# Moving exponentials, transposes and a split of maxima in the first batch of an mLSTM and Fourier-mixing kernel

## The chip, the cores and the metric

The kernel runs on one core of a Trainium2 chip. The metric is device microseconds of one execution. Single executions of this kernel on one core have no neighbour to be compared with, so all runs quoted are those that the measurement calls fast (none was called slow); the granted clock of TensorE is quoted beside a time where it matters. It is the mean over the span, 1.0 being full speed.

## The reference

The kernel computes two blocks in a row: an mLSTM cell over 768 tokens, and a Fourier mixing block with a two-layer MLP.

```python
B, H, S, D = 4, 8, 768, 40                       # d_model = H * D = 320
for t in range(S):                               # mLSTM cell
    m_new  = np.maximum(f_gate[:, :, t] + m, i_gate[:, :, t])
    f_stab = np.exp(f_gate[:, :, t] + m - m_new)
    i_stab = np.exp(i_gate[:, :, t] - m_new)
    C = f_stab * C + i_stab * outer(v_t, k_t)
    n = f_stab * n + i_stab * k_t
    y[:, :, t] = sigmoid(o_gate_t) * (C @ q_t) / np.maximum(np.abs(n @ q_t), 1.0)
# ... heads are joined: x is (4, 768, 320)
mixed = np.real(np.fft.fft(np.fft.fft(x, axis=1), axis=2))
u  = x + mixed
un = (u - mean(u)) / np.sqrt(var(u) + 1e-06)
out = u + np.maximum(un @ w_ch1, 0.0) @ w_ch2
```

## The kernel before

The mLSTM is computed in chunks of 128 tokens, six for each of the four batches. Within a chunk the recurrence becomes products: a chunk's output is (queries times the state C of the chunks before) plus (a 128x128 matrix of weighted scores times the values), and the state C is then carried on. The order in which each engine's instructions are issued is a hand-made plan: `at(slot, phase, function, ...)` puts a function at a slot, and within a slot smaller phases come first (`FILL` is 1, `FILL_PE` is 3). In the first batch (b = 0) chunk c begins at slot 3c.

```python
def spread_max(b, c, h0):            # TensorE: maxima and mask of four heads into PSUM, pM
    ...
def mlstm_exp(b, c, h0):             # ScalarE: four exponentials, W <- pM
    for h in range(h0, h0 + NP):
        nc.scalar.activation(out=k.W[:, h, :], in_=M, func=AF.Exp, scale=-1.0, bias=...)
def mlstm_scores(b, c): ...          # TensorE: ps
def mlstm_weigh(b, c): ...           # VectorE: W <- ps * W
def mlstm_from_state(b, c): ...      # TensorE: ph <- qg, C   ("state products")
def mlstm_from_chunk(b, c): ...      # TensorE: ph <- W, values
def mlstm_to_state(b, c): ...        # TensorE: pc, what the chunk adds to C
def mlstm_gather(b, c):              # ScalarE: the copies
    for hip in range(2):
        nc.scalar.copy(out=Cv, in_=k.pc[r])          # C of the next chunk, b == 0
    nc.scalar.copy(out=k.hT[r], in_=k.ph[r])         # h (cut: reversed and shifted forms)
    nc.scalar.activation(out=k.so, in_=k.so, func=AF.Tanh, scale=0.5)
def mlstm_turn(b, c, early): ...     # TensorE: transposes of h, px
def mlstm_finish(b, c): ...          # VectorE: x of the chunk, from px
# ...
def parts(s):                        # the split of the maxima into three bf16 parts, M3
    m, rest_ = M[0:BH, s], shift[:, s]
    nc.scalar.copy(out=M3[0:BH, s], in_=m)
    nc.vector.tensor_tensor(out=rest_, in0=m, in1=M3[0:BH, s], op=OP.subtract)
    nc.scalar.copy(out=below[:, s], in_=rest_)
    nc.scalar.copy(out=M3[BH:2 * BH, s], in_=rest_)
    nc.vector.tensor_tensor(out=M3[2 * BH:, s], in0=rest_, in1=below[:, s], op=OP.subtract)
# ...
def idle_products(n, ps=ps_s, tag="ps"):   # scratch products that only keep TensorE busy
    pw = ps.tile([L, 2 * L], FP, name="pi", tag=tag)
    for i in range(n):
        nc.tensor.matmul(pw, rest[:, 0:L], rest, start=True, stop=True, skip_group_check=True)
# ... the plan of a batch (cut)
at(s, FILL, mlstm_exp, b, c, 0)
at(s + 1, FILL - 0.5, mlstm_exp, b, c, NP)
at(s, FILL_PE + 2, mlstm_scores, b, c)
at(s + 2, FILL, mlstm_weigh, b, c)
at(s + 3, FILL_PE, mlstm_from_state, b, c)
at(s + 3, FILL_PE + 3, mlstm_from_chunk, b, c)
at(s + 3, FILL_PE + 3, mlstm_to_state, b, c)
at(s + 4, FILL, mlstm_gather, b, c)
```

After the chunks, `mix_fold` (VectorE, tile fe) and `mix_seq` (TensorE, tile pz) begin the Fourier transform. Pieces of the MLP's weights are converted along the way (`take`, `convert`, `join`, of which `convert` is ScalarE's, tiles e and m).

## Time and profile before

| | before |
|---|---|
| time, median of 4 runs | 463.84 us (463.58 to 464.18) |
| profiled run, another execution | 465.65 us, span 463.9 us, mean granted clock 0.985 |
| end of the first batch's mLSTM: last pz of part 0, profiled run | 60.23 us |
| mean granted clock of runs near 463.8 us (13 of 25 in the later calls) | 0.991 to 0.993 |
| half clock before 70 us, profiled run | 10.24 us, from 18.51 |

In the views PE is TensorE, PEld its weight loads, ACT ScalarE, DVE VectorE and POOL GpSimd; L470 is line 470 of the kernel. The page of the kernel before has these two rows: TensorE's busy tenths and the tenths of full clock granted, in 40 slices of 11.6 us.

```profile
PE   8688679999899999999999899999999999999997
PEclk9779999999999999999999989999999999999999
```

But for two eights and the last slice, all of TensorE's row that is not 9 lies in the first six slices, and slices two and three have a lowered clock.

The timeline of TensorE (columns: start us, busy us, engine, line, operation, tiles, form, count) gives the rhythm of the state products: 21.16, then 30.93, 37.49 and 44.04.

```profile
21.16 2.02 PE L470 MATMUL ph<-qg,C 128*128 128x128 f32 x8
30.93 1.11 PE L470 MATMUL ph<-qg,C 128*128 128x128 f32 x8
37.49 1.11 PE L470 MATMUL ph<-qg,C 128*128 128x128 f32 x8
44.04 1.11 PE L470 MATMUL ph<-qg,C 128*128 128x128 f32 x8
60.23 1.56 PE L631 MATMUL pz<-ds_sb,fe 128*128 128x385 f32 x4 [0.93 <-DVE fe L596]
```

The first group takes 2.02 us and the others 1.11 us for the same eight products: that is the half clock of chunk 1. What ScalarE does at a turn-around shows in its own timeline. The eight exponentials of chunk 2 are done long before the copies, so the copies of C start the moment pc is there (the bracket is ScalarE's own idle time, which costs nothing here):

```profile
22.03 2.18 ACT L412 ACTIVATE W<-pM,colT 128x128 f32<-128x128 f32 x8
28.20 0.62 ACT L502 COPY C<-pc 40x164 f32<-40x164 f32 x2 [4.00 <-PE pc L492]
28.84 0.59 ACT L515 COPY h<-ph 128x512 f32<-128x512 f32 x1
```

### The profile page before, as it was taken

What the parts mean: (1) busy time and instruction counts of PE and PEld (TensorE: products, weight loads), DVE (VectorE), ACT (ScalarE), POOL (GpSimd) and SP (SyncE); (2) the same over time, 40 slices, a digit from 0 to 9 for tenths busy, and PEclk for the clock granted to TensorE, in tenths of its full rate; (3) what the DMA queues carried; (4) which work ended last, traced back from release to release, by engine and by line L of the source; (5) the groups of instructions that cost most, each with busy time, mean ns of one, the idle gap of its engine ahead of it and who ended that gap; (6) DMA issues with size and microseconds to landing.
All of it is one profiled execution on the core that took longest, in us unless ns stands there. A gap on an engine that the chain in (4) does not pass through costs nothing.

```text
span 463.9 us, 7230 instructions
## 1 busy us (share of the span) xinstructions
PE 440.3 (95%) x2710; PEld 291.1 (63%) x2710; DVE 226.4 (49%) x582; ACT 154.7 (33%) x415; POOL 87.9 (19%) x129
## 2 busy tenths in 40 slices
PE   8688679999899999999999899999999999999997
PEld 6576435576567777766665467775664566466464
DVE  8568776859994336576301753346501640130110
ACT  7857247665442232352003442234001210200100
POOL 4344101434531431022001044302000000000000
PEclk9779999999999999999999989999999999999999
DMA  7488926259455244000067134300000000000000
GB/s 241 139 267 284 288 82 198 70 191 297 125 155 167 60 145 144 29 1 2 14 200 229 66 87 144 107 12 1 14 30 1 0 15 30 0 14 30 0 14 28
DMA packets 19566, 45.49 MB, mean 98 GB/s; under 512 B 2588, under 2 KB 9116, under 8 KB 19404
## 3 DMA queue, kind: packets, MB, share of 16 engines
q1 hardware_dynamic: 19532, 45.04, 31.2%
q8 instruction: 21, 0.34, 0.3%
q14 instruction: 13, 0.11, 0.1%
HBM read 40.92 MB, written 4.11 MB: 97 GB/s over the span
## 4 chain that ended last, share of the span: by engine, by line
PE 84%; DVE 8%; ACT 3%; issue 3%; POOL 1%; DMA 1%; POOLq 0%; ACTq 0%; DVEq 0%
PE po L783 28%; PE pm L761 21%; PE pm L765 6%; PE ps L456 4%; PE ph L477 4%; PE pu L662 4%; PE ph L470 4%; PE pz L631 3%; PE px L526 2%; PE put L702 2%; PE pzt L631 1%; PE pc L487 1%; PE pM L210 1%; DVE W L462 1%; ACT W L412 1%
## 5 line engine op out<-in xcount | busy, mean ns | idle before, releaser
L783 PE MATMUL po<-w_sb,hT 128*128 128x320 f32 x480 | 133.5, 435 | 0.0
L761 PE MATMUL pm<-uT,w_sb 128*128 128x384 f32 x320 | 119.1, 503 | 1.2 <-ACT uT L707 0.6
L783 PEld LDWEIGHTS po<-w_sb,hT 128*128 128x128 f32 x480 | 89.9, 190 | 39.4 <-issue 3.5
L761 PEld LDWEIGHTS pm<-uT,w_sb 128*128 128x128 f32 x320 | 56.9, 192 | 40.6 <-issue 10.1
L789 DVE SCALAR_TENSOR_TENSOR ot<-po,rstd,u 128x320 f32<-128x320 f32 x24 | 13.2, 551 | 84.0 <-PE po L783 84.0
L773 DVE TENSOR_SCALAR hT<-pm 128x384 f32<-128x384 f32 x35 | 19.4, 555 | 60.4 <-PE pm L765 60.1
L775 ACT ACTIVATE hT<-pm 128x384 f32<-128x384 f32 x45 | 21.5, 491 | 77.7 <-PE pm L765 77.7
L412 ACT ACTIVATE W<-W,colT 128x128 f32<-128x128 f32 x144 | 44.9, 395 | 0.0
L434 POOL TENSOR_SCALAR_AFFINE_SELECT W<-W 128x1024 f32<-128x1024 f32 x18 | 20.5, 1138 | 98.1 <-ACT W L412 68.0
L765 PE MATMUL pm<-uT,w1t_sb 64*128 64x384 f32 x160 | 36.6, 535 | 0.0
L707 ACT COPY uT<-put 128x384 f32<-128x384 f32 x24 | 11.5, 479 | 67.2 <-PE put L702 67.1
L462 DVE TENSOR_TENSOR W<-ps,W 128x512 f32<-128x512 f32 x48 | 30.7, 680 | 5.8 <-POOL W L434 5.7
L456 PE MATMUL ps<-qk 40*128 40x128 f32 x384 | 29.1, 290 | 0.4 <-DVE W L462 0.3
L456 PEld LDWEIGHTS ps<-qk 40*128 40x128 f32 x384 | 24.6, 193 | 5.0 <-issue 1.2
L422 POOL TENSOR_TENSOR qg<-qk,Gb 128x512 f32<-128x512 f32 x19 | 26.2, 1380 | 3.6 <-DMA Gb<-G_d 3.5
L477 PE MATMUL ph<-W,kvt 128*41 128x128 f32 x384 | 26.7, 283 | 0.0
L765 PEld LDWEIGHTS pm<-uT,w1t_sb 64*128 64x128 f32 x160 | 12.0, 184 | 21.8 <-issue 21.8
L470 PEld LDWEIGHTS ph<-qg,C 128*128 128x128 f32 x160 | 20.9, 198 | 5.8 <-issue 2.6
L428 POOL TENSOR_TENSOR vw<-kvt,colT 128x328 f32<-128x328 f32 x20 | 16.8, 840 | 36.2 <-DMA kvt<-in_kv 29.4
L470 PE MATMUL ph<-qg,C 128*128 128x128 f32 x160 | 22.9, 288 | 0.3 <-DVE x L541 0.3
L477 PEld LDWEIGHTS ph<-W,kvt 128*41 128x41 f32 x384 | 20.1, 120 | 3.1 <-issue 0.2
L526 PE MATMUL px<-ident,h 128*128 128x128 f32 x96 | 15.0, 279 | 4.8 <-ACT h L519 2.8
(140 smaller groups left out, 467.7 us busy)
## 6 DMA issues: line engine op xcount, KB each, us to landing
W<-M_d SPq DMA_DIRECT2D x18, 512.0 KB
kvt<-in_kv SPq DMA_DIRECT2D x24, 324.0 KB
qk<-in_qkT SPq DMA_DIRECT2D x48, 160.0 KB
raw<-in_w SPq DMA_DIRECT2D x10, 640.0 KB
so<-in_o SPq DMA_DIRECT2D x24, 160.0 KB
out<-ot SPq DMA_DIRECT2D x24, 160.0 KB
Gb<-G_d SPq DMA_DIRECT2D x38, 80.0 KB
ds_sb<-in_dft_s SPq DMA_DIRECT2D x1, 1155.0 KB
```

What stands on the lines that cost most here:

```text
L412: nc.scalar.activation(out=k.W[:, h, :], in_=M, func=AF.Exp, scale=-1.0, bias=colT[:, c, 0, b * H + h:b * H + h + 1])
L422: nc.gpsimd.tensor_tensor(out=k.qg, in0=k.qk[:, 0], in1=k.Gb, op=OP.mult)
L434: nc.gpsimd.affine_select(out=W, in_=W, compare_op=OP.is_ge, fill=0.0, base=0, pattern=[[0, H], [1, L]], channel_multiplier=-1)
L456: nc.tensor.matmul(k.ps[hip][:, p, :], k.qk[r, 1, p, :], k.qk[r, 0, p, :], start=True, stop=True)
L462: nc.vector.tensor_tensor(out=Wv, in0=k.ps[hip], in1=Wv, op=OP.mult)
L470: nc.tensor.matmul(k.ph[:, p, :], k.C[:, p, :], k.qg[:, p, :], start=(p == 0), stop=False, skip_group_check=True)
L477: nc.tensor.matmul(k.ph[hip * 64:hip * 64 + D1, p, :], k.v1[:, 2 * p + hip, :], k.W[:, 2 * p + hip, :], start=(c == 0 and p == 0), stop=Tr ...
L526: nc.tensor.transpose(k.px[:, p, :], k.hT[:, p, :], ident)
L761: nc.tensor.matmul(k.pm[i], w1_sb[:, ch, f0:f0 + L], u[2 * ch], start=(ch == 0), stop=False)
L765: nc.tensor.matmul(k.pm[i], w1t_sb[r, f // 2 * L:(f // 2 + 1) * L], u[1][r], start=False, stop=True)
L775: nc.scalar.activation(out=ht, in_=k.pm[f % 2], func=AF.Relu, scale=-1.0)
L783: nc.tensor.matmul(k.po, k.h[gr][f][:, i * L:(i + 1) * L], w2_sb[:, f, :], start=(f == 0), stop=(f == NFF - 1))
```

## The change

The intent is to use ScalarE's idle time under a chunk's products: the exponentials of a later chunk are put ahead of the copies, with two weight conversions; the transposes px go behind the next chunk's products and x behind the weighing, so that neither stands in front of work that the next products need; and the split of the maxima goes behind the exponentials of chunk 1, so that TensorE gets its first decays (pd) sooner. The arithmetic is the same, only order changes.

```diff
--- before.py
+++ after.py
@@ -210,11 +210,13 @@
                 nc.tensor.matmul(k.M[-1][:, h - h0, :], w.to_broadcast([w.shape[0], L]), x, start=False, stop=True,
                                  skip_group_check=True)
 
-        def parts(s):
+        def parts(s, second):
 
             m, rest_ = M[0:BH, s], shift[:, s]
-            nc.scalar.copy(out=M3[0:BH, s], in_=m)
-            nc.vector.tensor_tensor(out=rest_, in0=m, in1=M3[0:BH, s], op=OP.subtract)
+            if not second:
+                nc.scalar.copy(out=M3[0:BH, s], in_=m)
+                nc.vector.tensor_tensor(out=rest_, in0=m, in1=M3[0:BH, s], op=OP.subtract)
+                return
             nc.scalar.copy(out=below[:, s], in_=rest_)
             nc.scalar.copy(out=M3[BH:2 * BH, s], in_=rest_)
             nc.vector.tensor_tensor(out=M3[2 * BH:, s], in0=rest_, in1=below[:, s], op=OP.subtract)
@@ -298,9 +300,10 @@
         at(9, FILL + 0.9, maxima_out)
         for c in range(2, NT):
             for h0 in (0, NP):
-                at(3 * c - 1, FILL_PE + 2, spread_max, 0, c, h0)
+                at(3 * c - (1 if c == 2 else 3), FILL_PE + (2 if c == 2 else 3.7), spread_max, 0, c, h0)
         at(2, FILL + 0.5, columns_late)
-        at(2, FILL + 0.6, parts, last)
+        at(4, FILL - 0.45, parts, last, False)
+        at(4, FILL - 0.35, parts, last, True)
         at(4, FILL - 0.4, decay_late)
         at(4, FILL + 0.5, decays)
         at(5, FILL - 0.5, decays_out)
@@ -551,8 +554,9 @@
                 at(t, FILL + 0.2, mlstm_load_decay, b, c)
                 at(s, FILL, mlstm_load_o, b, c)
             if (b, c) > (0, 0):
-                at(s, FILL, mlstm_exp, b, c, 0)
-                at(s + 1, FILL - 0.5, mlstm_exp, b, c, NP)
+                ahead = b == 0 and c > 2
+                at(s - 2 if ahead else s, FILL - 0.5 if ahead else FILL, mlstm_exp, b, c, 0)
+                at(s - 2 if ahead else s + 1, FILL - 0.5, mlstm_exp, b, c, NP)
                 at(s, FILL_PE + 2, mlstm_scores, b, c)
                 if b > 0:
                     at(s + 1, FILL, mlstm_mask, b, c)
@@ -564,9 +568,9 @@
             at(s + 3, FILL_PE + 3, mlstm_from_chunk, b, c)
             at(s + 3, FILL_PE + 3, mlstm_to_state, b, c)
             at(s + 4, FILL, mlstm_gather, b, c)
-            t = s + (8, 8, 7, 5, 5, 5)[c]
-            at(t, FILL_PE + 1, mlstm_turn, b, c, b == 0 and c < 4)
-            at(t + 1, FILL, mlstm_finish, b, c)
+            t = s + ((9, 9, 6, 6, 6, 5) if b == 0 else (8, 8, 7, 5, 5, 5))[c]
+            at(t, FILL_PE + (3.5 if b == 0 and c < NT - 1 else 1), mlstm_turn, b, c, b == 0 and c < 4)
+            at(t + 1, FILL + 0.05, mlstm_finish, b, c)
 
 
     class Mix:
@@ -841,7 +845,7 @@
     plan_batch(2, 50, 79, s_mlp + 2 * MLP_SLOTS)
     plan_batch(3, 82, 111, s_mlp + 3 * MLP_SLOTS)
 
-    when = [((s, 0.7), (s + 2, 0.5), (s + 3, 0.6)) for s in (2, 5, 11)]
+    when = [((2, 0.7), (4, 0.5), (5, 0.6)), ((5, 0.7), (7, -0.3), (8, 0.6)), ((11, 0.7), (13, -0.3), (14, 0.6))]
     when += [((22, 0.7), (23, 0.7), (27, 0.6)), ((27, 0.7), (28, 0.7), (32, 0.6))]
     when += [((s, 0.7), (s + 1, 0.7), (s + 2, 0.6)) for s in (33, 36, 39, 42, 45)]
     pieces = w1_pieces + w2_pieces
```

Line numbers after the change are higher by two to four: pd is L289 before and L291 after, the state products are L470 and L473, the exponentials L412 and L415, the copies of C L502 and L505, the last pz L631 and L635.

## The prediction

> **What bounds the kernel now.** I read the page first. TensorE is busy 440.3 of 463.9 us, and the chain that ended last is 84% TensorE. After about 70 us the products of the MLP are back to back. The change touches only the first batch (0 to 62 us), so I cut the busy time into stretches, and there TensorE has holes. The next view is that one: busy time per engine in stretches (columns: stretch, length, then busy time of PE, PEld, DVE, ACT, POOL, then granted clock, DMA share and GB/s). The stretches are cut to the 3.41 us steps in which the clock changes.
>
> ```profile
> 15.13:18.54 3.41, 0.22 (x12) 0.10 (x6) 1.66 (x5) 3.40 (x14) 0.00 (x0) 1.00 0.10 33
> 18.54:21.95 3.41, 3.11 (x16) 2.41 (x17) 2.22 (x5) 3.34 (x7) 1.49 (x4) 0.50 0.27 66
> 21.95:25.37 3.42, 3.42 (x26) 2.96 (x27) 3.35 (x6) 2.23 (x9) 0.88 (x1) 0.50 0.85 253
> 25.37:28.78 3.41, 2.78 (x36) 2.09 (x32) 1.21 (x2) 0.55 (x2) 1.79 (x5) 0.50 0.96 265
> ...
> 264.30:267.71 3.41, 1.10 (x8) 0.56 (x5) 3.25 (x12) 3.23 (x8) 1.76 (x3) 1.00 0.02 7
> 267.71:271.13 3.42, 3.42 (x6) 1.76 (x6) 0.91 (x2) 0.81 (x2) 2.36 (x4) 0.50 0.37 105
> ```
>
> TensorE did 0.22 us in one step, ran at half clock for the next three, and needed 10.2 us to recover. Later, 1.10 us of work in a step was also followed by half clock. No step with 1.99 us or more was.
>
> What made the first hole, and the rhythm afterwards, is in the chain of waits in order of time (start, us, what):
>
> ```profile
> 13.31 0.60 DVE shift L217
> 13.93 0.62 ACT below L218
> 14.57 0.62 ACT M L219
> 15.20 2.18 ACT W L412 x8
> 17.38 1.11 ACT g L236 x4
> 18.51 0.29 DVE dec L285
> 18.84 0.71 PE pd L289 x2
> ...
> 34.77 0.29 ACT C L502
> 35.09 0.30 ACT C L502
> 35.41 0.58 ACT h L508
> 35.99 0.08 ACT h L519
> 36.12 0.66 PE px L526 x4
> ```
>
> So the first hole comes because ScalarE runs the split of the maxima, then eight exponentials, then the decays g, which TensorE needs for pd. From chunk 2 on each chunk has one period: products, then the copies of C and h on ScalarE, then px, then the spread of the maxima, then the next products. The timeline gives the starts of the state products (ph, L470) of chunks 2, 3 and 4 as 30.93, 37.49 and 44.04: a period of 6.55 us, of which 3.79 us is products up to the end of pc and 2.76 us the turn-around. The same view shows that pz waits 2.28 us until 50.11, for fe on VectorE, and the second half of the batch's pz (part 0) starts at 60.23.
>
> **What the Trainium skill says.** "TensorE: Matmul & The Clock Gate", Part 1 (What's actually happening), gives two clock states, full and half, set by a free-running window of 3413 ns: an idle window halves the clock. The trace agrees on the step (10.24 us at 0.50 is three of them). It differs in two ways: a window with 1.10 us of work also halved it, and coming back took three windows although the first two were busy for 3.11 and 3.42 us. The same page, Part 1 (Architectural detail), says that ScalarE and VectorE queues are strictly first in, first out, so a waiting instruction holds all behind it. The trace shows just that: the exponentials of chunk 2, ready or not, start at 22.03 behind the weight conversion. This is what decides the case.
>
> **The change part by part.** It adds and removes no arithmetic; one of three filler products near 24 to 26 slots falls elsewhere at most. I compared the built order of each engine.
>
> (a) Split of the maxima behind the exponentials of chunk 1. In the trace wk ends at 11.47, and the casts occupy ScalarE to 15.2 with 1.95 us idle inside. Now the eight exponentials run from 11.4 to about 13.5 (2.18), the cast of M to 14.0 (0.60), g to 15.2 (1.26). VectorE's difference (0.67) hides beside g. The two further casts end at 16.4 (0.62 each). VectorE takes the third part (0.68, to 16.4), qg (0.69, to 17.05), dec (0.28), so pd starts near 17.3 instead of 18.84: 1.5 us earlier. TensorE's hole shrinks from 3.49 to about 1.95 us, which should often escape the half clock. That is worth more: pd to pc of chunk 1 took 19.5 to 28.15 at half clock. The state products took 1.95 instead of 1.04, scores 2.01 instead of 1.09, chunk products 1.86 instead of 1.0, pc 1.1 instead of 0.6, spreads 1.67 instead of 0.88, in all about 4 us more. Chunk 1's products then end near 22.25 instead of 28.15: **5.9 us gained**.
>
> (b) Exponentials of chunk c+2 ahead of the copies of chunk c. On TensorE the spread of c+2 still stands behind the products of c, and on ScalarE its eight exponentials now stand before the copies of C(c+1) and h(c). The next state products need both copies (C as weights, and the buffer of ph). So the turn-around becomes: half the spread 0.44 and 0.1 latency, exponentials 2.18, C copies 0.62, h copies 0.66: about 4.0 us, plus what is put before it. For chunk 2 a weight conversion (0.82 + 0.72, about 1.5) also stands before the copies: 5.3 against 2.8, a loss of 2.5. For chunk 3, px (0.5) stands ahead of the spread: 4.45, a loss of 1.7. For chunk 4, two px (1.0) and a conversion (1.5): 6.4, a loss of 3.65. Together **7.85 us lost**.
>
> (c) px of chunk 3 behind the products of chunk 4, x and fold after it: 0.5 + 1.6 + 1.1 = 3.2 instead of 2.27 to pz: **0.9 lost**. px of chunk 4 now comes behind chunk 5's products. Before, x (1.6) and fold (1.5) of chunk 4 ran beside those products, and from the state products of chunk 5 (53.66) to the last pz (60.23) took 6.57. Now: products 2.0, px 0.6, x 1.6, fold 1.5, x of chunk 5 1.6, fold 1.25 = 8.55: **2.0 lost**.
>
> (d) x behind the weighing: VectorE is not what the next products wait for in most chunks any more; I count nothing. The tables' load is issued after x of chunk 0; it was issued at 37.3, and its semaphore had let a later issue go by 46.75. Even 5 us later it lands before pz needs it.
>
> Sum without new clock drops: -5.9 + 7.85 + 0.9 + 2.0 = **+4.85 us**, or about 468.7.
>
> (e) New holes. By (b) TensorE idles about 4.5 us before the state products of chunk 2, 3.2 before chunk 3 and 4.6 before chunk 4. In 4.5 us any phase of the window leaves one window with at most 1.16 us of work, close to the 1.10 that halved the clock. Each stage of products at half clock costs about 3.3 to 4 us (the sums of (a)). Estimated from the trace: chance 0.9, 0.6 and 0.85, times some 3 us with partial coverage, is about 7 us. Together about +12; I take off a little because windows may recover sooner, as at 271.13, where one was enough: **+11, so 475**.
>
> **The rivals.** First rival: the author's intent holds, ScalarE's idle time under the products (waits of 4.0, 1.5, 1.96 and 1.55 us before the C copies) is filled with exponentials, and the copies are ready sooner. For it: that idle time exists. Against: the spread that feeds the exponentials is still issued after the products, so they cannot start in it. It would give 457 to 461. Second rival: the holes stay at full clock, or only one drops; then 467 to 472. Third rival: the clock stays low from 25 to 60 us, every stage at half rate: 480 to 486. A fourth, that the tables' DMA takes the place of the waits (its share was about 1.0 from 42 to 50), would put pz later than 53 but I give it little. Nothing after 62 us is changed, and its engines take their work in order behind the first batch, so I carry the shift to the end one to one, with a microsecond or two of noise from where clock windows fall.
>
> **Range and chances.** Predicted 475.0 us. The low end, 466, is the plain sum with 2.5 us of luck; the high end, 484, is the third rival's middle. Slower by over 2% means above 473.1, which needs about 4.4 us of clock losses beside the plain sum, one to one and a half stages: chance 0.58. Within 2%: 0.38. Faster by over 2% (below 454.6) would need (b) to be no loss at all: 0.04.
>
> **What would show it.** In the changed profile: pd starts at 17.3 and full clock holds through chunk 1 (right on (a)); the wait of TensorE's ph (L473) for ScalarE appears as its longest wait, 4 to 5 us, with exponentials and then C copies just ahead in the chain (right on (b)); steps at clock 0.50 between 25 and 60 us (right on (e)); last pz of part 0 at 65 to 75 instead of 60.23. Wrong if TensorE's turn-around stays near 2.8 us, if the clock stays at 1.00 through holes of over 4 us, or if the stretch behind 62 us absorbs part of the shift.

## More of the kernel before

The groups of waits of TensorE in the first 62 us (columns: what waited, for what; then total us, times, longest us) say why it idles there:

```profile
PE pd L289 <- DVE dec L285: 3.5, 1, 3.5
PE px L526 <- ACT h L519: 2.8, 2, 1.4
PE pz L628 <- issue: 2.3, 1, 2.3
```

## The result, and the profile after

The changed kernel took **484.56 us** (median of 4 runs, 481.70 to 486.25) against 463.84 us (463.58 to 464.18) of the kernel before on the same chip. The ratio is 1.044, 95% interval 1.0386 to 1.0494: slower. A ratio here is the mean time of one kernel's fast runs over the mean of the other's of the same rounds, so it is not quite the ratio of the medians that are quoted. The profiled run took 483.68 us, with a span of 482.0 us and a mean clock of 0.965; the other three had 0.953 to 0.968. The direction was predicted; the size lies half a microsecond above the predicted range.

The same two rows of the page after, in slices of 12.05 us:

```profile
PE   8868677899989999999999989999999999999997
PEclk9877779999999999999999989999999999999999
```

The lowered clock now covers slices two to six. TensorE's groups of waits in the first 85 us:

```profile
PE ph L473 <- issue: 9.7, 3, 3.7
PE pz L632 <- issue: 3.1, 1, 3.1
PE pz L635 <- DVE fe L600: 3.0, 2, 2.2
PE pd L291 <- DVE dec L287: 2.2, 1, 2.2
```

The wait for pd shrank from 3.5 to 2.2 us. The waits of px for h are gone but for 0.2 us, and in their place stands a wait that there was not before: the state products, three times, 9.7 us together. The profile calls it "issue", not ScalarE. The same line has three semaphore instructions of 4.2 to 5.6 us on TensorE's queue ahead of these products. The Trainium skill says that an instruction with more than one engine to wait for may have such instructions put ahead of it ("Perfetto Trace Analysis", Identifying Dependency Chains); the trace agrees, and "issue" is read here as a wait for several engines. Which one came last is read from the timelines. TensorE's:

```profile
18.15 0.44 PE L291 MATMUL pd<-dec,spread_sb 32*128 32x80 f32 x2 [2.22 <-DVE dec L287]
19.52 2.02 PE L473 MATMUL ph<-qg,C 128*128 128x128 f32 x8
29.53 2.04 PE L473 MATMUL ph<-qg,C 128*128 128x128 f32 x8 [3.74 <-issue]
40.32 2.05 PE L473 MATMUL ph<-qg,C 128*128 128x128 f32 x8 [2.33 <-issue]
52.63 1.32 PE L473 MATMUL ph<-qg,C 128*128 128x128 f32 x8 [3.67 <-issue]
78.03 1.56 PE L635 MATMUL pz<-ds_sb,fe 128*128 128x385 f32 x4 [0.74 <-DVE fe L600]
```

and ScalarE's around the turn-around of chunk 2:

```profile
25.44 2.18 ACT L415 ACTIVATE W<-pM,colT 128x128 f32<-128x128 f32 x8 [2.46 <-PE pM L210]
27.46 0.88 ACT L345 ACTIVATE e<-e,ebias 128x640 uint32<-128x640 uint32 x1
28.18 0.78 ACT L346 ACTIVATE m<-m 128x640 f32<-128x640 uint32 x1
28.80 0.63 ACT L505 COPY C<-pc 40x164 f32<-40x164 f32 x2
29.45 0.59 ACT L518 COPY h<-ph 128x512 f32<-128x512 f32 x1
```

ScalarE sat idle for 2.46 us, waiting for the spread pM, which TensorE only makes after the products of the chunk; then it ran the eight exponentials and the conversion, and only then the copies of C, though pc had ended at 24.79. The copies end at 29.43 and the state products start at 29.53. In the next two turn-arounds they also start 0.1 us after the copies of C (40.22 and 52.53). The copy of h is not waited for: it still runs when the products start.

The last view is busy time in stretches, cut where the clock changes (columns: stretch, length, busy time of PE, PEld, DVE, ACT and POOL, then granted clock, DMA share, GB/s). The tenth column says it: in the first batch every full-clock stretch is followed by a stretch at 0.50.

```profile
15.90:19.30 3.40, 1.18 (x12) 0.83 (x11) 2.23 (x5) 3.28 (x7) 0.22 (x2) 1.00 0.32 85
19.34:22.70 3.36, 3.36 (x24) 3.14 (x22) 3.20 (x5) 3.33 (x11) 2.12 (x3) 0.50 0.81 239
22.76:29.50 6.74, 3.03 (x54) 2.24 (x53) 3.61 (x7) 4.24 (x14) 1.98 (x5) 1.00 0.96 299
29.60:36.40 6.80, 6.80 (x60) 5.79 (x60) 1.30 (x2) 0.87 (x3) 2.32 (x3) 0.50 0.25 82
36.40:39.80 3.40, 1.59 (x16) 1.12 (x14) 2.52 (x6) 2.22 (x9) 1.45 (x2) 1.00 0.00 0
39.85:46.60 6.75, 6.28 (x58) 5.73 (x60) 2.42 (x4) 1.37 (x5) 3.26 (x4) 0.50 0.81 285
46.70:53.40 6.70, 3.02 (x33) 2.38 (x28) 5.32 (x14) 4.81 (x14) 1.04 (x2) 1.00 0.70 254
53.50:60.20 6.70, 6.46 (x59) 4.97 (x57) 1.60 (x4) 1.14 (x6) 2.54 (x2) 0.50 0.84 288
60.30:63.60 3.30, 0.55 (x2) 0.30 (x2) 3.09 (x10) 0.37 (x2) 0.52 (x3) 1.00 0.94 265
63.75:70.50 6.75, 6.37 (x24) 4.31 (x26) 0.63 (x2) 0.00 (x0) 1.03 (x2) 0.50 0.17 47
```

TensorE idles in the full-clock stretches and does its products in the half-clock ones: 30.7 us at half clock in all, against 10.24 us before.

The medians differ by 20.7 us, the two profiled spans by 18.1: the profiled run before is 1.8 us slower than its median, the one after 0.9 us faster than its own. The 18.1 us can be laid out piece by piece, from the ends and starts in the timelines (each term to some 0.03 us):

| piece | before, us | after, us | difference |
|---|---|---|---|
| end of chunk 1's pc, from the start | 28.15 | 24.79 | -3.36 |
| three turn-arounds, end of pc to next state products | 2.78 + 2.77 + 2.75 | 4.74 + 3.81 + 5.59 | +5.84 |
| product stages of chunks 2, 3, 4 | 3.79 each | 6.98 + 6.72 + 6.28 | +8.61 |
| end of chunk 4's pc to first pz | 2.29 | 4.14 | +1.85 |
| first pz to state products of chunk 5 | 3.55 | 4.80 | +1.25 |
| state products of chunk 5 to last pz of part 0 | 6.57 | 10.18 | +3.61 |
| from there to the end | 403.71 | 403.95 | +0.24 |

The sum is +18.04 us. The largest term is not a wait but the same products at half the clock.

### The profile page after: what moved, and what is told of

It is laid out like the page before. It is cut to its first block, busy times and chain, and to the rows that moved or that the text cites. A ratio compares the mean times of both kernels' runs of the same rounds, so it can differ in the third digit from the quotient of the medians.

```text
span 482.0 us, 7223 instructions
## 1 busy us (share of the span) xinstructions
PE 450.3 (93%) x2710; PEld 298.8 (62%) x2710; DVE 227.0 (47%) x582; ACT 154.7 (32%) x415; POOL 90.2 (19%) x129
## 4 chain that ended last, share of the span: by engine, by line
PE 83%; DVE 8%; issue 3%; DMA 2%; ACT 2%; POOL 1%; SPq 0%; DVEq 0%; POOLq 0%
PE po L787 27%; PE pm L765 20%; PE pm L769 6%; PE ps L459 5%; PE ph L480 5%; PE ph L473 5%; PE pu L666 3%; PE pz L635 3%; PE px L529 2%; PE put L706 2%; PE pzt L635 1%; PE pc L490 1%; PE pM L210 1%; DMA qk<-in_qkT 1%; DVE W L465 1%
## 5 line engine op out<-in xcount | busy, mean ns | idle before, releaser
L415 ACT ACTIVATE W<-W,colT 128x128 f32<-128x128 f32 x144 | 44.9, 394 | 0.0
L473 PE MATMUL ph<-qg,C 128*128 128x128 f32 x160 | 26.0, 314 | 11.3 <-issue 9.7
L473 PEld LDWEIGHTS ph<-qg,C 128*128 128x128 f32 x160 | 23.4, 219 | 17.7 <-issue 14.5
L465 DVE TENSOR_TENSOR W<-ps,W 128x512 f32<-128x512 f32 x48 | 30.7, 680 | 5.8 <-POOL W L437 5.7
L459 PE MATMUL ps<-qk 40*128 40x128 f32 x384 | 31.5, 307 | 0.4 <-DVE W L465 0.3
L459 PEld LDWEIGHTS ps<-qk 40*128 40x128 f32 x384 | 26.8, 208 | 5.3 <-issue 1.7
L480 PE MATMUL ph<-W,kvt 128*41 128x128 f32 x384 | 28.7, 296 | 0.0
L480 PEld LDWEIGHTS ph<-W,kvt 128*41 128x41 f32 x384 | 21.6, 127 | 3.7 <-issue 0.9
L511 ACT COPY h<-ph 128x508 f32<-128x508 f32 x12 | 6.9, 579 | 38.2 <-PE ph L480 38.1
```

The costliest lines, as they stand in the source:

```text
L459: nc.tensor.matmul(k.ps[hip][:, p, :], k.qk[r, 1, p, :], k.qk[r, 0, p, :], start=True, stop=True)
L465: nc.vector.tensor_tensor(out=Wv, in0=k.ps[hip], in1=Wv, op=OP.mult)
L473: nc.tensor.matmul(k.ph[:, p, :], k.C[:, p, :], k.qg[:, p, :], start=(p == 0), stop=False, skip_group_check=True)
L480: nc.tensor.matmul(k.ph[hip * 64:hip * 64 + D1, p, :], k.v1[:, 2 * p + hip, :], k.W[:, 2 * p + hip, :], start=(c == 0 and p == 0), stop=Tr ...
```

## The experiments

The theory after the result has two parts. **Turn-around:** the exponentials, fed by a spread that is still behind the products, hold the copies of C. **Clock:** the holes that this and the later px open make the clock halve, and that costs more than the holes. Rivals: the px and x moves cost the time and the exponentials do not; or the holes alone cost it and the clock is of little weight. Every kernel below gave correct results. The kernel before, run beside them, spread over 463.20 to 470.11 us, with a mean clock from 0.993 down to 0.974; 13 of these 25 runs lie near 463.8 us, at 0.991 to 0.993; they are called usual below. Differences below are from that 463.8 us unless a ratio is given.

### The split of the maxima alone

```diff
-        at(2, FILL + 0.6, parts, last)          # and parts cut in two, as in the change
+        at(4, FILL - 0.45, parts, last, False)
+        at(4, FILL - 0.35, parts, last, True)
```

> The kernel before with only the split of the maxima moved behind the exponentials of chunk 1. Theory (the split helps; the loss comes from the exponentials ahead of the copies and from the clock): pd starts about 0.7 to 1.5 us earlier, the hole ahead of it shrinks from 3.5 to about 2.2 us, the half clock after it lasts at most one or two windows, and the gain up to the end of chunk 1 is about 3.4 us as in the changed kernel: 460.4 us (459 to 462). Rival (the split is itself part of the loss): 464 us or more.

Measured: 463.47 us (463.43 to 463.61), ratio 0.9966 (0.9901 to 1.0031). The gain against the usual run did not come. In its stretches (columns as above) there is a reason:

```profile
15.87:19.28 3.41, 1.35 (x13) 1.03 (x14) 2.43 (x6) 3.29 (x8) 0.43 (x2) 1.00 0.34 92
19.28:26.11 6.83, 6.83 (x62) 5.70 (x60) 5.59 (x8) 3.44 (x10) 3.77 (x7) 0.50 0.92 269
```

TensorE still waited 2.23 us for pd, and the clock was half for two steps after it instead of the three of the profiled run before; a third one, of 3.41 us at 49.97, had no counterpart there. Against that profiled run the split did gain: its span is 461.8 instead of 463.9 us. Its clock was 0.989 in all four runs, below the usual run's; the one run of before at 0.989 took 464.92 us. So the split is harmless, but its hole did not keep the clock.

### The change with exponentials and conversions put back

```diff
-                at(s - 2 if ahead else s, ..., mlstm_exp, b, c, 0)
-                at(s - 2 if ahead else s + 1, FILL - 0.5, mlstm_exp, b, c, NP)
+                at(s, FILL, mlstm_exp, b, c, 0)
+                at(s + 1, FILL - 0.5, mlstm_exp, b, c, NP)
-    when = [((2, 0.7), (4, 0.5), (5, 0.6)), ((5, 0.7), (7, -0.3), (8, 0.6)), ((11, 0.7), (13, -0.3), (14, 0.6))]
+    when = [((s, 0.7), (s + 2, 0.5), (s + 3, 0.6)) for s in (2, 5, 11)]
```

> The changed kernel with the exponentials and the weight conversions put back behind the copies; split, px and x stay as changed. Theory (exponentials and conversions ahead of the copies are the main cause): the turn-arounds go back to about 3 us, no step between 25 and 45 us is at half clock, and the time is 464 us (461 to 467): minus 3.4 of the split, plus about 3 of px and x. Rival (px and x are the main cause): 475 us or more.

Measured: 470.96 us (468.24 to 472.33), ratio 1.0119 (1.0045 to 1.0194). Putting the exponentials back returns 13.6 of the 20.7 us, so they are the larger part, but not all: 7 us stayed where none was expected. In its profile, which is of its fastest run, TensorE waits 3.2 us for fe before the first pz, up to 1.7 us for qg of GpSimd and up to 1.8 us for W of VectorE.

### px and x alone

```diff
-            t = s + (8, 8, 7, 5, 5, 5)[c]
-            at(t, FILL_PE + 1, mlstm_turn, b, c, b == 0 and c < 4)
-            at(t + 1, FILL, mlstm_finish, b, c)
+            t = s + ((9, 9, 6, 6, 6, 5) if b == 0 else (8, 8, 7, 5, 5, 5))[c]
+            at(t, FILL_PE + (3.5 if b == 0 and c < NT - 1 else 1), mlstm_turn, b, c, b == 0 and c < 4)
+            at(t + 1, FILL + 0.05, mlstm_finish, b, c)
```

The new slots of the spread go with it.

> The kernel before with only px moved behind the next chunk's products and x behind the weighing. Theory (exponentials are the main cause, px and x cost 0.9 before the first pz and 2.0 after it): 467 us (465 to 470). Rival (px and x are the main cause): 475 us or more.

Measured: 473.42 us (472.24 to 473.56), ratio 1.0171 (1.009 to 1.0252). More than expected, and the waits for fe and W stand in TensorE's groups of waits of this kernel too (that for qg is 0.8 us here):

```profile
PE pz L628 <- DVE fe L596: 3.2, 1, 3.2
PE pz L631 <- DVE fe L596: 3.0, 2, 2.2
PE ps L456 <- DVE W L462: 2.1, 2, 1.8
```

The two waits for fe are the losses of point (c) of the prediction, now with half clock after them (3.41 us at 46.4 and 6.83 us at 53.2, which the kernel before did not have). The profile has the 10.24 us behind pd as well. The wait for W was not in the prediction: with px and x moved, the next products wait for VectorE's weighing.

### The exponentials alone

```diff
-                at(s, FILL, mlstm_exp, b, c, 0)
-                at(s + 1, FILL - 0.5, mlstm_exp, b, c, NP)
+                ahead = b == 0 and c > 2
+                at(s - 2 if ahead else s, FILL - 0.5 if ahead else FILL, mlstm_exp, b, c, 0)
+                at(s - 2 if ahead else s + 1, FILL - 0.5, mlstm_exp, b, c, NP)
```

The conversions ahead and the new slots of the spread go with it.

> The kernel before with only the exponentials (and the weight conversions that go with them) moved ahead of the copies; split, px and x as before. Theory (this part lengthens each turn-around by 1 to 2.8 us, and holes of that length halve the clock for the next products): turn-arounds of about 4.7, 3.8 and 5.6 us, half clock after at least two of them, 477 us (472 to 482). Rival (it hurts only together with the moved px and x): 467 us or less.

Measured: 477.53 us (473.91 to 477.70), ratio 1.0213 (1.0126 to 1.03), as expected; the kernel before of that call had a median of 465.43 us. From the timelines of ScalarE and TensorE:

```profile
26.64 2.17 ACT L412 ACTIVATE W<-pM,colT 128x128 f32<-128x128 f32 x8 [1.95 <-PE pM L210]
29.99 0.63 ACT L502 COPY C<-pc 40x164 f32<-40x164 f32 x2
31.35 1.12 PE L526 MATMUL px<-ident,h 128*128 128x128 f32 x4 [4.37 <-ACT h L519]
```

The hole is 4.37 us, ended by the copy of h behind those of C behind the exponentials. Four half-clock stretches stand in this run (3.41 us at 19.54, behind pd, then 10.24 at 29.78, 3.41 at 43.43, 10.24 at 53.67). The exponentials and conversions by themselves, with px and x as before, do this.

### The change with its holes filled

Scratch products were put at the ends of the product stages. They compute nothing that is used; they only keep TensorE busy while it would wait.

```diff
+    for s, n in ((3, 4), (6, 8), (9, 4), (12, 8), (15, 6)):
+        at(s, FILL_PE + 3.8, idle_products, n, ps_m, "pm")
```

> The changed kernel with filler products on TensorE in its five holes (ahead of pd, of the state products of chunks 2, 3 and 4, and of the first pz), which write a scratch bank nobody reads. Theory (the clock is the larger part of the loss: about 13 of 20.7 us): no half clock between 15 and 75 us, 471 us (468 to 475). Rival (the clock only accompanies the holes, the turn-arounds are the loss): 481 us or more, since the holes stay as long.

Measured: 469.97 us (469.62 to 470.43), ratio 1.0106 (1.0039 to 1.0173), with a clock of 0.996 in all four runs. Its stretches of 15 us, from 15 to 60:

```profile
15.00:30.00 15.00, 14.43 (x156) 11.82 (x154) 12.19 (x17) 12.16 (x33) 6.69 (x11) 1.00 0.76 235
30.00:45.00 15.00, 13.86 (x150) 11.53 (x147) 10.12 (x23) 8.25 (x27) 5.66 (x7) 1.00 0.65 229
45.00:60.00 15.00, 12.75 (x121) 9.64 (x119) 7.44 (x20) 2.93 (x9) 4.43 (x7) 1.00 0.85 271
```

This is the experiment that decides the size. With the clock held at 1.00 the changed order costs 6.1 us over the 463.84 of before, and the other 14.6 us (484.56 - 469.97) are the clock. The two come from different calls, but the fillers leave the turn-arounds about as long as they were (4.73, 3.80 and 6.03 us in this profile, 4.74, 3.81 and 5.59 above), and this kernel's runs differ by 0.8 us. An estimate from the stretches of the changed kernel agrees: TensorE was busy 29.3 us in those at half clock, and half of that is 14.6. The 463.84 of before has half clock of its own; against the split with four fillers (461.05 us, mostly at 0.996, below) the rest of the new order costs 8.9 us.

### What is left at full clock: conversions and exponentials

Two kernels take parts back from the filled one. The first returns the conversions behind the copies (fillers 4, 5, 4, 5, 6), the second returns the exponentials as well (fillers only at slots 3 and 15).

```diff
-    when = [((2, 0.7), (4, 0.5), (5, 0.6)), ((5, 0.7), (7, -0.3), (8, 0.6)), ((11, 0.7), (13, -0.3), (14, 0.6))]
+    when = [((s, 0.7), (s + 2, 0.5), (s + 3, 0.6)) for s in (2, 5, 11)]
```

> The changed kernel with its holes filled, and only the two weight conversions put back behind the copies. Theory (each conversion of 1.5 us ahead of the copies of chunks 2 and 4 lengthens that turn-around by its whole length): 467 us (466 to 468), against 470.0 with the conversions ahead. Rival (VectorE or a transfer is what these turn-arounds end on): 469.5 us or more.

> The changed kernel with exponentials and conversions behind the copies again, and filler only in the holes ahead of pd and of the first pz. Theory (at held clock the exponentials and conversions together cost about 5.8 us, the sum of the longer turn-arounds in the profile of the changed kernel): 464.5 us (463 to 466). Rival (at held clock the order of exponentials costs nothing, px and x do): 469 us or more.

Measured: 467.96 us (466.53 to 468.48, ratio 1.0073) for the first, so the conversions cost 2.0 us by the medians. That is not at full clock: in its profile half clock came back for 6.83 us at 58.6. Its two runs at a clock of 0.996 were 466.53 and 467.49, which makes it 2.5 to 3.4 us. The second took 466.96 us (465.44 to 470.04, ratio 1.0065) instead of 463 to 466: a miss, since its holes of 1.83 us (qg), 1.77 us (W) and 2.24 us (fe) left half clock at 41.8 and 58.9; its runs had a clock of 0.984 to 0.993. Its two at 0.993 were 465.44 and 466.09, so exponentials and conversions together are worth about 4 us there, but this pair doesn't settle the figure.

### Fillers without the change, and with the split

Can the filler help the kernel before? Seven fillers at slot 3 of it, and then the split with four:

```diff
+    for s, n in ((3, 7),):      # the first; the second is the split with ((3, 4),)
+        at(s, FILL_PE + 3.8, idle_products, n, ps_m, "pm")
```

> The kernel before with seven filler products (about 3 us at full clock) in the hole ahead of pd, nothing else. Theory (the hole of 3.5 us costs about 4 us only by halving the clock): full clock through chunk 1, 460 us (459 to 461.5). Rival (chunk 1 is bound by something beside TensorE, so the clock there is hidden): 463 us or more.

> The kernel before with the split behind the exponentials of chunk 1 and four filler products in the shorter hole ahead of pd. Theory (part a of the prediction is right once the clock holds: 1.3 us from the split, 4 from the clock): 458.5 us (457 to 460). Rival (the split gains nothing on top of the filler): 460 us.

Measured: 464.29 us (463.29 to 466.37), ratio 0.9959 (0.9891 to 1.0026), for the first, a miss. Its last product ended at 457.96 us against 460.5 in the profiled run before, so 2.5 us were gained in the products, but the output's tail took 4.5 us instead of 3.4, and it was no faster than the kernel before in that kernel's better runs on the chip (463.20 at 0.993). The expectation rested on a profile with more half clock (0.985) than the usual run: the filler's runs, at 0.993 to 0.994, are hardly above the usual 0.991 to 0.993, so there was little clock to gain. The rest of the miss stays open. The second: 461.05 us (460.38 to 461.67), ratio 0.9883 (0.982 to 0.9947), with full clock to 46.64 us and the last pz at 56.70 instead of 60.23. That is a smaller gain than expected (458.5) and a real one: its slowest run is below the fastest of all 25 of the kernel before (463.20).

### The spread ahead of the products too

If the exponentials fail because their input is issued late, then the spread of chunk c+2 should go ahead of the products of chunk c, so that the exponentials run beside them. This is the split with four fillers and:

```diff
-                at(3 * c - 1, FILL_PE + 2, spread_max, 0, c, h0)
+                at(3 * c - (1 if c == 2 else 3), FILL_PE + (2 if c == 2 else -0.5), spread_max, 0, c, h0)
+                early_exp = b == 0 and c > 2
+                at(s - 3 if early_exp else s, FILL_PE - 0.3 if early_exp else FILL, mlstm_exp, b, c, 0)
+                at(s - 3 if early_exp else s + 1, FILL_PE - 0.3 if early_exp else FILL - 0.5, mlstm_exp, b, c, NP)
```

with px of the early chunks in the middle of the products.

> Split and filler as in the run before, and the stated intent made possible: the spread of chunk c+2 stands ahead of the products of chunk c on TensorE, so its exponentials run on ScalarE beside those products and the copies find ScalarE free; px stands in the middle of the next products, conversions behind the copies as before. Theory (order ahead of the copies is good only if the input is there): turn-arounds under 2 us, a period of about 6 us, 456 us (453 to 459). Rival (exponentials anywhere ahead of the copies delay them): 462 us or more.

Measured: 462.92 us (461.77 to 464.49), ratio 0.9926 (0.986 to 0.9992). That is a miss: 456 was expected, and the split with its fillers alone took 461.05. The mechanism holds all the same: the state products of chunks 1, 2 and 3 start at 19.34, 24.59 and 29.84, a period of 5.25 us instead of 6.55. But the next engine is there at once, as TensorE's timeline shows:

```profile
32.39 1.75 PE L459 MATMUL ps<-qk 40*128 40x128 f32 x16 [1.44 <-DVE W L465]
```

Scores wait for VectorE's weighing, the clock halves at 34.9, and pz waits 2.76 us for fe. It shows that the intent can be met when the input is issued ahead too, not that it pays.

### The version that was best

The split, four fillers at slot 3 and four at slot 15 ahead of the first pz, exponentials and px where they were:

```diff
+    for s, n in ((3, 4), (15, 4),):
+        at(s, FILL_PE + 3.8, idle_products, n, ps_m, "pm")
```

> The split with its filler (as the run split_filled), and four more filler products in the 2.3 us hole ahead of the first pz. Theory (that hole halves the clock in some runs, worth about 1 us): 460.2 us (459.5 to 461.2), no half clock before 100 us. Rival (the filler delays pz by as much as the clock gains): 461 us or more.

Measured: 460.61 us (458.07 to 460.96, 7 runs), against 463.75 us (463.36 to 465.69, 11 runs), ratio 0.9921 (0.9901 to 0.9941). Six runs had a clock of 0.996 and one of 1.00; the last pz of the profiled run (458.07 us) is at 54.39. It beats both the kernel before and the changed one, by 0.8% and, from another call, by 4.9%. Its order is that of before but for the split, with the clock nearly held. What the second four fillers add to the first (461.05, another call) is not shown.

Taken singly against 463.8 us, the split gave -0.3, px and x +9.6 and the exponentials with the conversions +13.7: 23.0 together, against 20.7 for all. They needn't add up, since a step at half clock that one part has caused cannot be caused again by another.

## Why the prediction was wrong in size

**The mechanism and the direction were right.** Point (b) said that ScalarE's order would hold the copies, and where: the exponentials and then the copies of C stand just ahead of the state products in all three turn-arounds, and the exponentials with the conversions cost 10 us (by the ratio of their rounds) to 14 us (against 463.8). The profile names the wait "issue" where I had written that it would name ScalarE. The first rival, the intent, did not come, for the reason given against it. The size of (b) was 7.85 and is 5.84 us; the difference is three times 0.66 us, the copies of h, which I had said the products would wait for and which they did not. The fourth rival, the tables' transfer, was not tested; it was issued at 41.2, and the first pz (63.05) starts while VectorE writes fe (62.63 to 63.18), so nothing points to it.

**Point (a)** promised 5.9 us (its own terms add up to about 5.5) and gave 3.36 between the two profiles. The pd came at 18.15, not 17.3, and the hole of 2.22 us, which "should often escape the half clock", did not: the step from 19.30 was at 0.50. The split alone showed the same (2.23 us, then 6.83 us at half clock) and gained nothing against a usual run. A hole of the same length escaped only in the profile with the exponentials put back, so "often" was not borne out. With the clock held by fillers, pc of chunk 1 ends at 22.67, which is 5.5 us earlier.

**Point (c)** had two terms. To the first pz 0.9 was predicted and 1.85 came; behind the state products of chunk 5, 2.0 and 3.61, the latter partly at half clock. **Point (d)**, nothing for x behind the weighing, fits the changed kernel but not px and x by themselves, where scores waited 2.1 us for W. The shift behind 62 us was carried one to one, as predicted (+0.24).

**The step that failed is (e), "about 7 us", taken off to about 6.** The clock cost 14.6 us, twice as much. The plain sum of (a) to (d) was +4.85, and the filled kernel, with the clock held, measured +6.1; span against span of the two profiles (467.95 and 463.94) it is +4.01: -5.48 for (a), +6.25 for (b), +1.36 and +2.40 for (c), and -0.52 in the rest. That part was sound, with errors that in part cancel. Three things were too small in (e). First, I gave each of three holes a chance and "some 3 us with partial coverage", about 7 us. All three came, two steps each, and coverage was nearly whole: the half clock began at 29.54, 39.78 and 53.44, within 0.9 us of the starts of the products. It cost 3.19, 2.93 and 2.49 us in the three product stages, 8.61 together. Second, and this is the larger part, I counted no clock loss for the two holes of (a) and (c), at pd and before pz, and both had one: 3.41 us at half clock from 19.30 and 6.83 us from 63.67. The remaining 6 of the 14.6 us lie mostly there (half of the 3.36 and 6.37 us that TensorE was busy in them is 4.9, an estimate). Third, what I took off "because windows may recover sooner" rested on one step at 271.13 that had recovered after one window; in the first batch four of the five took two. What came is the third rival, every stage of products at half rate, to which I had given only the edge of the range.

Why a hole of 2.2 us was followed by half clock in some profiles and not in one can be read from the traces. Cut into the 3.41 us steps of the clock, the 13 profiles have 30 steps at full clock that were followed by one at half. All 25 steps with 1.45 us or less of TensorE's work were, four of the six with 1.52 to 1.70 us, and of those with 1.71 us or more a single one (2.37 us at 31.45, in the kernel with the spread ahead). In the first 85 us of the changed kernel the five had 1.19, 0.01, 1.62, 0.80 and 0.56 us. So what counts here is the work left in a step more than the length of the hole. With the exponentials put back, a step ended at 17.03, inside the hole ahead of pd, and the steps on both sides kept 2.61 and 1.99 us.

What stays open is that one step, and why recovery takes one, two or three steps. The kernel before spread by 1.5%, with clocks that fell as the times rose; where the steps stand when the kernel starts is a likely reason, but no run here controlled it.

## What to carry to other kernels

Put an instruction ahead in an in-order queue only when its input is issued ahead as well; else it waits there, and everything behind it waits with it. When a change opens a hole on TensorE, ask how much work is left in each step of the clock around it (here 1.45 us or less of 3.41 always brought half clock), count the products behind such a hole at double their time for one to three steps, and judge an order of instructions by a version whose holes are filled with scratch products, so that order and clock are told apart. Here the split with the old holes filled gained 3.1 us (460.61 against 463.75), and the whole new order lost 20.7.

## What the Trainium skill lacked or had wrong

- "TensorE: Matmul & The Clock Gate", Part 1 (HAM oscillation) gives as rule that TensorE must have no idle gaps over about 3.4 us. Here gaps of 2.2 us were enough: windows with 1.18 and 1.35 us of work were followed by 0.50, though TensorE's longest gap in them was 2.22 and 2.23 us. In the filled kernel with the exponentials put back a gap of 1.77 us, ahead of ps at 40.81, was enough, in a window with 1.5 us of work. A gap of 2.22 us that the end of a window cut in two was not. Coming back, for which its Part 1 (What's actually happening) asks for at least one busy window, took one, two or three windows of 3.41 us, and the page does not say which: 3.41 us at 19.30 in the changed kernel, 6.83 us at 29.54, 39.78, 53.44 and 63.67, and 10.24 us at 18.51 in the kernel before.
- No page says that a profile can show a wait for several engines without naming any of them. Here the 9.7 us that ended with ScalarE's copies of C stood under "issue", with semaphore instructions of 4.2 to 5.6 us ahead of the products.
